# A second queue for the QKV weight loads, a K product tile by tile, ten warm-ups for eighteen, and a new order on every engine

## The chip, the core and the metric

The kernel runs on one core of one Trainium2 chip. The metric is the device time of one execution in microseconds (us). The kernel before was run three times; the number to compare with is the median. One more execution was profiled, and all rows of the profile come from that one.

Five engines work side by side, each through its own queue in order: TensorE (PE, with its weight loads PEld), VectorE (DVE), ScalarE (ACT), GpSimd (POOL) and SyncE (SP), which here only issues DMAs. An instruction that waits holds up everything behind it on its engine.

## The reference

Two rounds of one attention layer and one MLP layer with the same weights in both rounds, on x of 1 x 2048 x 512 (S = 2048 rows, D = 512), all in bf16:

```python
    x = A_x
    x = x + _A_ref(_layernorm(x, axis=-1), A_wqkv, A_wo)
    x = x + _B_ref(_layernorm(x, axis=-1), B_w1, B_b1, B_w2, B_b2)
    x = x + _A_ref(_layernorm(x, axis=-1), A_wqkv, A_wo)
    x = x + _B_ref(_layernorm(x, axis=-1), B_w1, B_b1, B_w2, B_b2)
```

`_A_ref` projects to q, k and v with wqkv (512 x 1536), takes 32 heads of 16, lets each row see itself and the 255 rows before it, takes the softmax, multiplies by v and projects with wo. `_B_ref` is gelu(x w1 + b1) w2 + b2 with 1792 hidden columns.

## The kernel before, in words

The rows are cut into tiles of 128, and the two rounds together give 32 tiles ("tau", 0 to 31), or 16 attention blocks of two tiles ("b", 0 to 15; 0 to 7 is the first round). X stays in SBUF for the whole kernel. All weights are loaded once.

For each block, `lnq` (L672) normalizes its two tiles: statistics on DVE (`bs`, `ba`, L616 and L618), the variance plus eps (`vp`, L622, on POOL or DVE), a power on POOL (`pw`, L628), and the scaling on DVE (`xn`, L638). The normalized tile is transposed into xnTA, for the first four tiles and the last two by PE (`tp`, L650) with a copy out of PSUM on ACT or DVE (`te`, L605 to L607), and otherwise by a DMA transpose on SP (`tx`, L643). Then `proj` (L684) makes Q and K (`q0_0` is block 0, first half of the columns; each such product is four nodes of two matmuls of 256 columns, 128x256), and `kv` (L691) copies K to KT with a mask on DVE (`ke`, L698) and makes V (`v`, four matmuls of 512 columns for a tile). Q and V are copied by DVE or ACT (`qe`, `ve`, L605 to L607). Two DMAs on SP shift V by half a tile (`vs`, L713).

`attention` (L741) works in "visits" of 512 score columns for four row groups: scores on PE (`sc`, L765), two exponentials of 128x1024 on ACT (`ex`, L772), masks on DVE or POOL (`mk`, L793). A block has ten visits (five at the start of a round), 150 in all. Then come the product with V (`pv`, L817), a transpose, a reciprocal and a scaling (`od`, `rc`, `nm`, L826 to L834), another transpose (`ot`, L840) and the output projection (`op`, L861, added to X by `rs`, L866). `mlp` (L870) works in jobs of two or four tiles: W1 products (`m`), a bias on DVE and a gelu on ACT (`gb`, `ga`) or both on ACT (`ge`, L897), the W2 products (`y`) and the sum into X (`ya`, L909). Exponentials and gelus need different tables on ACT; each change of table is a load of 1.28 us.

The code records about 3,080 "nodes" with what each reads and writes (`_Plan.add`, L391). What runs in which order is written out by hand: `_ORDER` (L167) lists all nodes in one order, which gives the order on each engine; `_ALT` (L323) names the nodes that run on their second engine (a copy on ACT instead of DVE, a mask on POOL instead of DVE); `_TURNS` (L342) adds pairs in which one node has to wait for another; `_BANKS` (L362) gives each product its PSUM bank. `_Sched.op` (L62) turns each node into an instruction with semaphore waits. DMAs take turns on eight semaphores (L73 to L79), and a DMA on a semaphore waits until the one before it there has landed.

The loads at the start all stand on SP. In the recorded order they are issued as: X tile 0, X tile 1, X tiles 2 and 3, K weights first half (256 KB), b1, Q weights first half, X tiles 4 to 7 (512 KB), K weights second half, V weights (512 KB), Q weights second half, X tiles 8 to 11, X tiles 12 to 15, b2, Wo. W1 and W2 come later, between other DMAs.

Eighteen warm-up matmuls of 128x512 on a tile of zeros (L555 to L558) keep PE busy: fifteen of them before the first projection product, the other three between the products of blocks 0 and 1.

## Time and profile before

| | us |
|---|---|
| median of three runs | 440.32 |
| lowest and highest of them | 439.97 and 440.69 |
| the profiled execution | 440.62 |
| its span in the profile | 438.9 |
| PE busy, ACT busy, DVE busy, POOL busy in it | 424.2, 385.6, 341.0, 201.1 |

How to read it: times in rows are microseconds from the start of the span, and the means of one instruction are nanoseconds. A row of the timeline has its start, its length, the engine, the line of the kernel, the operation, the tile it writes and those that it reads, the count, and in brackets the idle time of the engine ahead of it with what ended it. A row of a group has its total busy time and the mean of one, then the idle time ahead of the group with what ended most of it. The profile's granted clock (PEclk) is 1.00 in all stretches but the last one of 20 us (0.97). PE's busy time holds the latency of each matmul too, so that a PE busy 100% isn't a PE at its peak.

### The profile page before, as it was taken

What the parts mean: (1) busy time and instruction counts of PE and PEld (TensorE: products, weight loads), DVE (VectorE), ACT (ScalarE), POOL (GpSimd) and SP (SyncE); (2) the same over time, 40 slices, a digit from 0 to 9 for tenths busy, and PEclk for the clock granted to TensorE, in tenths of its full rate; (3) what the DMA queues carried; (4) which work ended last, traced back from release to release, by engine and by line L of the source; (5) the groups of instructions that cost most, each with busy time, mean ns of one, the idle gap of its engine ahead of it and who ended that gap; (6) DMA issues with size and microseconds to landing.
All of it is one profiled execution on the core that took longest, in us unless ns stands there. A gap on an engine that the chain in (4) does not pass through costs nothing.

```text
span 438.9 us, 16940 instructions
## 1 busy us (share of the span) xinstructions
PE 424.2 (97%) x7579; PEld 230.4 (52%) x7579; DVE 341.0 (78%) x647; ACT 385.6 (88%) x457; POOL 201.1 (46%) x224
## 2 busy tenths in 40 slices
PE   8989999999699989999999999999999999999997
PEld 4555756554344554454455555454564554544763
DVE  5999987799686889876899797877877686754852
ACT  3899999999999899999999988899888979899632
POOL 4366136464550275451854437743454515625222
PEclk9999999999999999999999999999999999999999
DMA  7772912002200102311030211201232022101011
GB/s 236 210 203 50 227 39 56 15 21 64 48 1 14 32 16 48 50 33 25 10 74 9 37 29 27 52 1 33 58 45 69 1 33 63 47 0 28 15 48 49
DMA packets 47972, 23.25 MB, mean 53 GB/s; under 512 B 33180, under 2 KB 47900, under 8 KB 47900
## 3 DMA queue, kind: packets, MB, share of 16 engines
q1 hardware_dynamic: 47900, 22.17, 21.8%
q8 instruction: 60, 0.98, 0.9%
q14 instruction: 12, 0.10, 0.1%
HBM read 8.00 MB, written 2.10 MB: 23 GB/s over the span
## 4 chain that ended last, share of the span: by engine, by line
PE 84%; ACT 8%; DVE 4%; DMA 3%; issue 1%; SPq 1%; POOL 0%; DVEq 0%
PE ps L664 65%; PE ps L765 10%; PE ps L817 8%; ACT E L772 7%; DMA W_sb<-in_B_w_dram 1%; DMA xnTB<-xn 1%; DVE stat L616 1%; DVE OD L826 1%; DVE KT L698 1%; DMA X<-in_A_x_dram 0%; PE ps L650 0%; DVE xn L638 0%; DVE X L909 0%; DVE X L866 0%; SPq L643 0%
## 5 line engine op out<-in xcount | busy, mean ns | idle before, releaser
L772 ACT ACTIVATE E<-ps 128x1024 bf16<-128x1024 f32 x300 | 283.2, 1040 | 25.6 <-PE ps L765 24.8
L793 POOL TENSOR_TENSOR E<-E,mask 128x512 bf16<-128x512 bf16 (+2 forms) x114 | 120.3, 1069 | 132.5 <-ACT E L772 52.7
L664 PE MATMUL ps<-W_sb,gT 128*128 128x512 bf16 x448 | 114.8, 380 | 0.1
L664 PE MATMUL ps<-xnTB,W_sb 128*128 128x512 bf16 (+1 forms) x560 | 109.3, 337 | 1.9 <-ACT E L772 1.5
L664 PEld LDWEIGHTS ps<-xnTB,W_sb 128*128 128x128 bf16 x560 | 51.9, 98 | 43.4 <-issue 4.6
L664 PE MATMUL ps<-xnTA,Wqkv_sb 128*128 128x256 bf16 x512 | 71.6, 273 | 1.2 <-ACT E L772 0.9
L765 PE MATMUL ps<-QT,KT 32*128 32x128 bf16 (+3 forms) x1920 | 60.4, 231 | 4.6 <-ACT E L772 2.6
L664 PEld LDWEIGHTS ps<-W_sb,gT 128*128 128x128 bf16 x448 | 39.4, 98 | 42.8 <-issue 4.0
L793 DVE TENSOR_TENSOR E<-E,mask 128x512 bf16<-128x512 bf16 (+2 forms) x122 | 51.0, 445 | 13.8 <-ACT E L772 11.6
L664 PEld LDWEIGHTS ps<-xnTA,Wqkv_sb 128*128 128x128 bf16 x512 | 46.6, 98 | 22.6 <-issue 3.3
L765 PEld LDWEIGHTS ps<-QT,KT 32*128 32x128 bf16 x1920 | 28.4, 92 | 52.6 <-ACT E L772 34.5
L826 DVE STREAM_TRANSPOSE OD<-ps 128x1024 f32<-128x1024 f32 x32 | 40.0, 1249 | 16.5 <-PE ps L817 14.6
L897 ACT ACTIVATE gT<-ps,b1T 128x512 bf16<-128x512 f32 (+1 forms) x80 | 43.0, 606 | 9.1 <-PE ps L664 9.0
L889 DVE TENSOR_SCALAR gT<-ps,b1T 128x512 bf16<-128x512 f32 (+1 forms) x60 | 36.7, 631 | 11.9 <-PE ps L664 11.4
L616 DVE BATCH_NORM_STATS2 stat<-X 128x6 f32<-128x512 bf16 x64 | 43.6, 687 | 3.0 <-DMA X<-in_A_x_dram 2.2
L905 POOL TENSOR_TENSOR Xb<-X,b2all 128x512 f32<-128x512 bf16 x32 | 36.8, 1154 | 13.1 <-DVE X L909 6.4
L817 PE MATMUL ps<-E,Va 64*17 64x256 bf16 (+3 forms) x1920 | 41.0, 230 | 1.8 <-DVE Va L605 0.5
L698 DVE TENSOR_TENSOR KT<-ps,parmask 128x1024 bf16<-128x1024 f32 x32 | 38.7, 1213 | 5.2 <-PE ps L664 5.0
L817 PE MATMUL ps<-E,Vs 64*17 64x192 bf16 (+3 forms) x1920 | 42.2, 230 | 0.0
L628 POOL TENSOR_TENSOR rstd<-rstd,mhalf 128x2 f32<-128x2 f32 (+1 forms) x33 | 24.2, 734 | 27.6 <-DVE rstd L622 23.3
L817 PEld LDWEIGHTS ps<-E,Va 64*17 64x17 bf16 x1920 | 29.2, 84 | 11.9 <-issue 8.3
L664 PE MATMUL ps<-Wo_sb,OT 128*128 128x512 bf16 x128 | 35.3, 380 | 0.1
(51 smaller groups left out, 350.1 us busy)
## 6 DMA issues: line engine op xcount, KB each, us to landing
Vs<-Va SPq DMA_DIRECT2D x64, 68.0 KB, 2.7
W_sb<-in_B_w_dram SPq DMA_DIRECT2D x4, 512.0 KB, 4.6
out_dram<-X SPq DMA_DIRECT2D x16, 128.0 KB, 1.8
X<-in_A_x_dram SPq DMA_DIRECT2D x3, 512.0 KB, 7.9
Wqkv_sb<-in_A_wqkv_dram SPq DMA_DIRECT2D x4, 256.0 KB, 5.5
W_sb<-in_B_w_dram SPq DMA_DIRECT2D x1, 768.0 KB, 5.2
W_sb<-in_B_w_dram SPq DMA_DIRECT2D x2, 384.0 KB, 5.0
Wqkv_sb<-in_A_wqkv_dram SPq DMA_DIRECT2D x1, 512.0 KB, 7.7
```

The source lines that it names most:

```text
L616: add("dve", lambda e, B, t=t, k6=k6: e.bn_stats(stat6[:, k6, :], X[:, t, :]), reads=["X%d" % t], writes=["st%d" % k6], key="bs%d" % (k + j))
L628: add("pool", lambda e, B, j=j, n=n: e.tensor_tensor(out=rstd[:, k + j : k + j + n], in0=rstd[:, k + j : k + j + n], in1=mhalf[:, 0:n], op ...
L664: r = e.matmul(ps[:, B[g][0], cols], lhsT, rhs, start=st, stop=sp)
L698: add("dve", lambda e, B, g=g, i=i: e.tensor_tensor(out=KT[:, kb, 2 * i : 2 * i + 2].rearrange("p c m a q -> p a (c m) q"), in0=ps[:, B[g] ...
L765: x = e.matmul(ps[:, bk[r], o : o + n], KT[rows, kb, c, m].rearrange("p a q -> p (a q)"), QT[rows, c, q : q + n], start=True, stop=True)
L772: add("act", lambda e, B, g_=g_, gi=gi: e.activation(E[:, 2 * gi : 2 * gi + 2, e0 : e0 + 512], ps[:, B[g_][0] : B[g_][0] + 2, :], AF.Exp, ...
L793: fn = lambda e, B: e.tensor_tensor(out=Ew, in0=Ew, in1=Mw, op=ALU.mult)
L817: x = e.matmul(ps[32 * r : 32 * r + VW, B[g][par], c % 2 * 2 * P + lo : c % 2 * 2 * P + hi], V[rows, (2 * b + m // 2) % VR, c * HC + 2 * r ...
L826: add("dve", lambda e, B: e.transpose(OD[:, s].rearrange("p a c q -> p (a c q)"), ps[:, B[g][0] : B[g][0] + 2, :]), reads=["ps:" + g], wri ...
L889: add("dve", lambda e, B, g=g, fc=fc: e.tensor_scalar(out=gT[:, fc, c0 : c0 + M], in0=ps[:, B[g][0], 0:M], scalar1=b1T[:, fc : fc + 1], sc ...
L897: add("act", lambda e, B, g=g, fc=fc: e.activation(gT[:, fc, c0 : c0 + M], ps[:, B[g][0], 0:M], AF.Gelu_apprx_tanh, bias=b1T[:, fc : fc + ...
L905: add("pool", lambda e, B, t=t, xs=xs: e.tensor_tensor(out=Xb[:, xs, :], in0=X[:, t, :], in1=b2all[:], op=ALU.add), reads=["X%d" % t, "b2a ...
```

## The change

Four things are changed together.

First, `load_w` puts the five QKV weight loads on ACT's queue. In the new order they are K first half, Q first half and K second half, all three ahead of ACT's first table load; then Q second half between the copies `te0` and `te1`; then V between `te1` and `te3`. Each has a semaphore of its own (`actdma0` and so on), so that none waits for an earlier one; the K load first waits for the memset of gT. SP now issues X tile 0, tile 1, tiles 2 and 3, tiles 4 to 7, b1, tiles 8 to 11, tiles 12 to 15, b2, Wo.

Second, the first K product (`k0_0`) is cut by tile: four nodes of four matmuls with 128 columns, of which the first two need tile 0 of xnTA alone. `k0_0` now comes ahead of `q0_0`, whose products in before stood in between.

Third, NWARM is 10: eight warm-ups ahead of the first transposes, one after each of the first two tiles' transposes, and none later.

Fourth, `_ORDER`, `_ALT`, `_TURNS` and `_BANKS` are replaced. At the start, DVE now has the statistics of tiles 2 and 3 ahead of `xn1`, and the statistics of tile 4 (`bs4`) ahead of the copy `te2`. By engine: copies of Q on ACT 8 for 11, copies of V on ACT 15 for 14; masks on DVE 127 for 122, on POOL 109 for 114; `nm` on POOL 15 for 13; `vp` on POOL 22 for 16. Both orders have 18 table loads on ACT.

```diff
-    COUNTERS = ("pe", "act", "dve", "pool") + tuple("spdma%d" % i for i in range(8))
+    N_ACT_DMA = 8
+    COUNTERS = ("pe", "act", "dve", "pool") + tuple("spdma%d" % i for i in range(8)) + tuple("actdma%d" % i for i in range(8))
...
         if dma:
-            assert eng == "sp"
-            counter = "spdma%d" % (self.dma_rr % self.N_DMA_SEMS)
-            self.dma_rr += 1
             inc = 16
-            prev = self.cnt_val[counter]
-            if prev > 0:
-                need(counter, prev)
+            if eng == "act":
+                assert self.act_dma < self.N_ACT_DMA
+                counter = "actdma%d" % self.act_dma
+                self.act_dma += 1
+            else:
+                assert eng == "sp"
+                counter = "spdma%d" % (self.dma_rr % self.N_DMA_SEMS)
+                self.dma_rr += 1
+                prev = self.cnt_val[counter]
+                if prev > 0:
+                    need(counter, prev)
...
-    NWARM = 18
+    NWARM = 10
...
-        def dma(fn, writes, reads=(), key=None):
-            return add("sp", fn, reads=reads, writes=writes, dma=True, key=key)
+        def dma(fn, writes, reads=(), key=None, eng="sp"):
+            return add(eng, fn, reads=reads, writes=writes, dma=True, key=key)
...
-                ["Wqkv%d_%d" % (which, i) for i in range(2) if lo <= D // 2 * i < lo + n], key="ldw%d_%d" % (which, lo))
+                ["Wqkv%d_%d" % (which, i) for i in range(2) if lo <= D // 2 * i < lo + n],
+                reads=["g0_0"] if (which, lo) == (1, 0) else (), key="ldw%d_%d" % (which, lo), eng="act")
...
-        def proj(g, which, i, xs, xr, war):
+        def proj(g, which, i, xs, xr, war, first=False):
+            if first:
+                for n in range(4):
+                    j, half = divmod(n, 2)
+                    kc = 2 * i + half
+                    pe_group(g, [(Wqkv_sb[:, dc, which * D + kc * P : which * D + (kc + 1) * P],
+                                  xnTA[:, xs, dc, j * P : (j + 1) * P],
+                                  slice(half * 256 + j * P, half * 256 + (j + 1) * P), dc == 0, dc == DC - 1)
+                                 for dc in range(DC)],
+                             DC, [xr[j], "Wqkv%d_%d" % (which, i)], fresh=(n == 0), war=war, key=g, k0=n)
+                return
...
-                proj(g, 1, i, xs, xr, names)
+                proj(g, 1, i, xs, xr, names, b + i == 0)
```

## The prediction

> **What bounds the kernel now.** I read the page's busy shares first, then its chain of waits, then a table by stretches, then the costliest groups.

> ```profile
> PE 424.2 (97%) x7579; PEld 230.4 (52%) x7579; DVE 341.0 (78%) x647; ACT 385.6 (88%) x457; POOL 201.1 (46%) x224
> PE 84%; ACT 8%; DVE 4%; DMA 3%; issue 1%; SPq 1%; POOL 0%; DVEq 0%
> 0.00:20.00 20.00, 18.19 (x157) 10.04 (x157) 15.55 (x36) 11.58 (x15) 8.16 (x25) 1.00 0.81 237
> 20.00:40.00 20.00, 18.43 (x450) 10.86 (x450) 18.90 (x34) 19.52 (x24) 10.78 (x12) 1.00 0.50 133
> 100.00:120.00 20.00, 15.52 (x424) 8.78 (x427) 16.21 (x29) 19.28 (x23) 9.42 (x12) 1.00 0.27 58
> 380.00:400.00 20.00, 20.00 (x204) 8.70 (x187) 10.17 (x20) 19.30 (x24) 7.94 (x9) 1.00 0.01 2
> L772 ACT ACTIVATE E<-ps 128x1024 bf16<-128x1024 f32 x300 | 283.2, 1040 | 25.6 <-PE ps L765 24.8
> ```

> TensorE is busy 97% of the span and ScalarE 88%. The chain runs through PE for 84% and ACT for 8%. The stretches (columns: length, then busy time of PE, PEld, DVE, ACT, POOL, then granted clock, DMA share and GB/s) say where each rules. From 380 to 400 us PE has no idle time. From 100 to 120 us it lacks 4.48 us while ACT is busy 19.28 of 20. The 300 exponentials make up most of ACT's time. The chain in order of time says the same:

> ```profile
> 106.68 11.92 ACT E L772 x13
> 126.60 11.62 PE ps L664 x57
> 422.33 13.47 PE ps L664 x90
> ```

> Thirteen exponentials stand back to back in 11.92 us, 0.92 us each. So the first layer is led by ACT in places, and the end is bare PE work. Time is won only by starting the exponentials earlier, by taking work off ACT in the early stretches, or by taking work off PE.

> **The change part by part.** The base is the profiled execution: 440.62 us, of which 438.9 is the span. It lies 0.30 us above the median of 440.32, so I subtract from the median at the end.

> *The start.* The rows of before, in order of time:

> ```profile
> 0.79 1.34 SPq L565 DMA_DIRECT2D X<-in_A_x_dram  x3
> 1.24 4.29 PE L557 MATMUL ps<-gT 128*128 128x512 bf16 x10 [1.24 <-DVE gT L555]
> 2.81 0.69 DVE L616 BATCH_NORM_STATS2 stat<-X 128x6 f32<-128x512 bf16 x1 [1.63 <-DMA X<-in_A_x_dram]
> 4.24 2.32 SPq L570 DMA_DIRECT2D Wqkv_sb<-in_A_wqkv_dram  x3
> 6.11 1.08 ACT L607 ACTIVATE xnTA<-ps 128x512 bf16<-128x512 bf16 x2 [4.05 <-PE ps L650]
> 6.35 1.03 PE L557 MATMUL ps<-gT 128*128 128x512 bf16 x4
> 7.25 0.99 PEld L664 LDWEIGHTS ps<-xnTA,Wqkv_sb 128*128 128x128 bf16 x10 [0.37 <-ACT xnTA L607]
> 7.79 0.73 DVE L638 TENSOR_SCALAR xn<-X,statmv,rstd 128x512 bf16<-128x512 bf16 x2 [0.75 <-POOL rstd L628]
> 9.02 2.60 PE L664 MATMUL ps<-xnTA,Wqkv_sb 128*128 128x256 bf16 x22
> 9.22 0.42 DVE L605 COPY xnTA<-ps 128x512 bf16<-128x512 bf16 x1 [0.16 <-PE ps L650]
> 10.17 0.69 DVE L616 BATCH_NORM_STATS2 stat<-X 128x6 f32<-128x512 bf16 x1 [0.53 <-DMA X<-in_A_x_dram]
> 12.04 0.40 PE L765 MATMUL ps<-QT,KT 32*128 32x256 bf16 x8 [0.42 <-DVE KT L698]
> 12.60 0.59 PE L664 MATMUL ps<-Wqkv_sb,xnTA 128*128 128x512 bf16 x2
> ```

> The first projection product waits for ACT's copy of xnTA at 7.25, not for weights. So weights that come sooner free nothing there by themselves. ACT issues five loads: three ahead of its table load, one between the copies te0 and te1, one between te1 and te3. ACT is idle for 4.05 us before 6.11, which hides the first three (2.32 us for three is the longest such group on SP). The other two stand where ACT waits for the next transposes; I take 0 for them, up to 0.8 us if one takes long, as SP's three did.

> The tile-by-tile K product has 16 matmuls of 128 columns and as many weight loads, for 8 of 256. Ten loads took 0.99 us, 0.10 each, so eight more cost up to 0.8 us; half of them run while PE waits for tile 1 anyway, and the rest stands where the next wait is DVE's. I take 0.

> What decides is the new order on DVE. In before, tile 2's copy te2 (9.22) stands ahead of the statistics that wait for the load of tiles 4 to 7 (10.17). In after, such a statistic, bs4, stands ahead of te2, and PE's q1_0 and k1_0 (sixteen of the 22 matmuls of the 9.02 row, 16/22 x 2.6 = 1.9 us less the overlap of their ends, 1.75) wait for te2. The first scores come behind them. If that load is early, bs4 starts when xn2 and xn3 end, near 8.9 (xn1 now follows two statistics, so the row of 7.79 moves 0.4 back): scores at 8.9 + 0.69 + 0.42 + 1.75 = 11.76, or 0.3 us before the 12.04 of before. If the load lands at L, they come at L + 0.69 + 0.42 + 1.75.

> ```profile
> 0.00:9.00 9.00, 7.61 (x42) 3.74 (x43) 5.28 (x18) 2.59 (x4) 5.37 (x19) 1.00 0.72 212
> 4.70:6.50 1.80, 1.65 (x13) 0.78 (x12) 1.80 (x6) 0.39 (x1) 0.97 (x4) 1.00 0.66 160
> 9.00:11.60 2.60, 2.60 (x26) 1.99 (x23) 1.92 (x4) 1.57 (x3) 0.00 (x0) 1.00 1.12 342
> Wqkv_sb<-in_A_wqkv_dram SPq DMA_DIRECT2D x1, 512.0 KB, 7.7
> ```

> When it is saturated, the DMA moves 342 GB/s, 0.34 MB per us; from 4.70 to 6.50 only 160, as SP hadn't issued enough. In before, the load landed at 10.17 with 1.54 MB issued up to and with it. In after, 1.02 MB of SP's own stand there, and the 0.77 MB of ACT's first three loads share the engines: 1.79 MB, 0.25 MB or 0.75 us more; filling the gap of 4.70 to 6.50 gives back 1.8 x 0.18 / 0.34 = 0.95. So L = 10.0 and the scores start at 12.85: **0.8 us late**. Bounds: 0.3 early (load in time), 3.5 late (rival 1).

> [...]

> *Warm-ups.* Eight fewer. Five of them stood at the start, where PE waits. Three stood between the products of the first layer:

> ```profile
> 19.81 0.38 PE L557 MATMUL ps<-gT 128*128 128x512 bf16 x1
> 21.34 0.38 PE L557 MATMUL ps<-gT 128*128 128x512 bf16 x1
> 31.08 0.39 PE L557 MATMUL ps<-gT 128*128 128x512 bf16 x1
> ```

> Four in a row take 1.03 us with the last one's tail (row of 6.35), 0.22 each without it; three are 0.65. PE has 1.57 us of idle time from 20 to 40, which hides some of it: I take **-0.4** (bounds -0.65 and 0).

> *Searched order.* The recorded orders differ everywhere, yet engine by engine little is moved: 18 table loads in both, and nearly the same PE work ahead of each exponential. Copies move from ACT to DVE:

> ```profile
> L607 ACT ACTIVATE Va<-ps 128x512 bf16<-128x512 f32 x14 | 8.7, 623 | 0.3 <-PE ps L664 0.2
> L607 ACT ACTIVATE QT<-ps 128x512 bf16<-128x512 f32 x11 | 6.8, 619 | 0.8 <-PE ps L664 0.8
> L605 DVE CAST QT<-ps 128x512 bf16<-128x512 f32 x21 | 14.3, 682 | 5.2 <-PE ps L664 5.1
> L793 DVE TENSOR_TENSOR E<-E,mask 128x512 bf16<-128x512 bf16 (+2 forms) x122 | 51.0, 445 | 13.8 <-ACT E L772 11.6
> ```

> Ahead of the 50th exponential, ACT has 12 copies for 15, three by 0.62, 1.86 us less, all in the stretch where it is busy 19.5 of 20 or close to that. DVE takes them for 3 x 0.68 = 2.0 us; it was busy 18.90 of 20 from 20 to 40 us, so this is not free. I take **-1.4** (bounds -1.86 and 0), near the full sum, as ACT's share there is the higher one. Over the whole run ACT has two copies fewer; DVE gets five masks more, 5 x 0.445 = 2.2 us by the last row above, and gives six small variance steps to POOL. I cost these at 0, as DVE has 22% idle time over the span; if they all fell where it is busy 18.90 of 20, they would cost up to 2.2.

> What else the new order does to stalls can't be worked out from the trace. Its bounds are the 4.48 us of PE idle from 100 to 120 us, all closed or once more opened; I take 0.

> Sum: +0.8 - 0.4 - 1.4 = -1.0, that is 439.6 on the profiled execution, and from the median 440.32 - 1.0 = **439.3**. The bare PE work of the end (13.47 us) has the same matmuls in both.

> **The rivals.**

> 1. *V's weights come last (slower).* In after the V load (512 KB) is ACT's fifth, issued only behind te1, beside SP's 2.69 MB of X, b2 and Wo. PE meets its first V product right after the first scores (12.60 in before), and the second scores stand behind it. In before it landed 7.7 us after an issue near 4.75, at 12.45: just in time. If SP's loads are all served first, 3.97 MB stand up to it for 2.30 in before: 1.67 / 0.34 = 4.9 us more, less 0.95, so 4.0 later, 16.4. It costs nothing up to 13.4 (0.8 late like the scores), and from 15.3 on, 2.7 late, it outweighs the 1.8 us won and the bound of 0.9. At 16.2 the second scores are 3.6 late: 440.32 + 3.6 - 1.8 = 442.1. For it: two rings, and a load that is issued late. Against it: equal shares put it near 13.1. Chance 0.20.

> 2. *The new order closes holes.* If 60% of the 4.48 us goes, -2.7: 439.3 - 2.7 = 436.6. For it: PE idle there waits for ACT, which has less work. Against it: ACT is busy 19.28 of 20 in that very stretch. Chance 0.18.

> 3. *The clock.* The ten first warm-ups took 0.43 us each, the four from 6.35 0.22 each, though the granted clock in the rows is 1.00 throughout: PE doubles its pace after some 4.3 to 5 us of work. Eight warm-ups end at 1.24 + 8 x 0.43 = 4.7, and PE then idles until the first transposes. If the pace stays at half until the scores, 24 matmuls of 256 columns cost 0.11 us more each: 2.6 us, 439.3 + 2.6 = 441.9, slower too. [...] Chance 0.10.

> 4. *It does not do what it says.* The loads free nothing (row of 7.25), and DVE gives back what ACT saves, as the chain is PE's: +0.8 - 0.4 = 440.7. Chance 0.12.

> **How the numbers follow.** Forecast 439.3, chance 0.40, its own range 438.2 to 440.7 by the bounds of the copies and the start. Faster by over 0.2% means below 439.44, slower above 441.2; 0.2% is about what a measurement of this kernel can tell from no change. Faster: 0.24 of the forecast and rival 2's 0.18 = 0.42. Same: 0.16 of the forecast, 0.01 of rival 1, 0.06 of rival 4 = 0.23. Slower: 0.19 + 0.10 + 0.06 = 0.35. The range 436.4 to 442.6 leaves out the lower part of rival 2 (0.07) and the upper parts of rivals 1 and 3 (0.11).

> **What would show it.** Start: the first scores at 12.85, with te2 behind a statistic that waits for X; at 11.7 the load came early. Rival 1: the first V product waits for Wqkv_sb beyond 13.4. Rival 3: projection products of 128x256 spaced by 0.21 us instead of 0.11. Copies: the 50th exponential earlier by 0.8 us or more against the first. Rival 2: PE busy above 18 of 20 in every stretch from 80 to 180. I am wrong where stalls of several us stand in stretches that this text doesn't name.

## The result, and the profile after

The changed kernel takes **445.96 us** (median of six runs, 444.37 to 448.7), beside 440.5 for the kernel before on the same chip (439.65 to 442.5). The ratio is 1.0123 [1.0083, 1.0163]: 5.5 us slower, and outside the range of 436.4 to 442.6. The profiled execution took 444.37 us with a span of 442.5.

The page of the changed kernel: busy time, and the costliest group.

```profile
PE 423.7 (96%) x7579; PEld 230.7 (52%) x7579; DVE 341.3 (77%) x646; ACT 384.6 (87%) x455; POOL 199.1 (45%) x227
L790 ACT ACTIVATE E<-ps 128x1024 bf16<-128x1024 f32 x300 | 283.6, 1038 | 26.8 <-PE ps L783 26.0
```

The work is the same: as many matmuls as before, the same time in them, the same exponentials. So the 3.6 us that the span is longer by (442.5 for 438.9) are waits, or matmuls spaced further apart. The table by stretches of the changed kernel says where (length, busy PE, PEld, DVE, ACT, POOL, granted clock, DMA share, GB/s):

```profile
0.00:20.00 20.00, 14.65 (x106) 8.77 (x107) 12.89 (x31) 8.15 (x11) 8.19 (x23) 0.91 0.75 220
100.00:120.00 20.00, 16.52 (x487) 9.60 (x470) 17.54 (x33) 19.36 (x23) 9.90 (x12) 1.00 0.36 55
380.00:400.00 20.00, 20.00 (x254) 9.02 (x250) 13.18 (x24) 17.69 (x22) 5.78 (x6) 1.00 0.07 19
```

From 0 to 20 us PE is busy 14.65 us for 18.19, ACT 8.15 for 11.58, and the granted clock is 0.91 for 1.00. In the other two PE is as busy as before or busier, at a clock of 1.00. ACT's table loads are good milestones, since both kernels have 18 of them at the same places of the work. The second and the last, in before and then in the changed kernel:

```profile
46.22 1.28 ACT L897 ACT_TABLE_LOAD   x1
408.07 1.28 ACT L897 ACT_TABLE_LOAD   x1
49.52 1.28 ACT L915 ACT_TABLE_LOAD   x1
412.81 1.28 ACT L910 ACT_TABLE_LOAD   x1
```

That is 3.3 us late at 46 us and 4.7 at 408, and the span ends 3.6 late: nearly everything is lost before 46 us. The timeline of that start (start, length, engine, line, operation, tiles, count, and in brackets the idle time ahead with its releaser):

```profile
6.10 1.29 DVE L624 BATCH_NORM_STATS2 stat<-X 128x6 f32<-128x512 bf16 x2 [0.75 <-DMA X<-in_A_x_dram]
9.08 0.19 PE L597 MATMUL ps<-ident,b1raw 14*128 14x14 bf16 x1 [0.71 <-DMA b1raw<-in_B_b_dram]
9.20 1.89 PE L672 MATMUL ps<-xnTA,Wqkv_sb 128*128 128x128 bf16 x14
11.98 0.42 DVE L613 COPY xnTA<-ps 128x512 bf16<-128x512 bf16 x1 [1.25 <-PE ps L658]
14.33 0.40 PE L783 MATMUL ps<-QT,KT 32*128 32x256 bf16 x8
16.21 0.82 PE L672 MATMUL ps<-Wqkv_sb,xnTA 128*128 128x512 bf16 x3 [1.48 <-DMA Wqkv_sb<-in_A_wqkv_dram]
17.61 0.40 PE L783 MATMUL ps<-QT,KT 32*128 32x256 bf16 x8
```

Read it from the top. DVE waits until 6.10 for X tiles 2 and 3. Then PE, with the rest of the K product queued behind it, waits until 9.08 for b1, 3.5 KB. The next 14 matmuls (the last twelve of the K product, of 128 columns, and two of the Q product) take 1.89 us; in the run below with the loads back on SP the same 14 take 1.27. So te2 waits for PE's transposes, and not for a statistic. The first scores come at 14.33 for 12.04. Then V's weights land, at 16.2, and the second scores come at 17.61, where they stood at 13.78 before: 3.8 us late.

Two rows of a shorter table of the changed kernel, and landings in the DMA view (KB each, median us from issue to landing), V and X tiles 2 and 3 in the changed kernel, then X tiles 2 and 3 in before:

```profile
4.70:6.50 1.80, 0.75 (x7) 0.29 (x6) 1.01 (x4) 0.60 (x1) 0.88 (x2) 1.00 1.11 344
9.00:11.60 2.60, 2.52 (x22) 2.37 (x23) 1.42 (x4) 0.05 (x1) 0.26 (x1) 0.50 1.11 337
```

```profile
Wqkv_sb<-in_A_wqkv_dram ACTq DMA_DIRECT2D x1, 512.0 KB, 8.0
X<-in_A_x_dram SPq DMA_DIRECT2D x1, 256.0 KB, 4.4
X<-in_A_x_dram SPq DMA_DIRECT2D x1, 256.0 KB, 2.8
```

The gap that the prediction wanted filled is filled: 344 GB/s from 4.70 to 6.50 for 160. But X tiles 2 and 3, which took 2.8 us to land before, now take 4.4. And from 9.00 to 11.60 the granted clock is 0.50. In before the rows show 1.00 even over the slow first warm-ups (0.43 us each, for 0.22 from 6.35 on), and I had not counted on seeing a slow clock in them; here the row shows it.

### The profile page after: what moved, and what is told of

It reads as the page before. It is cut to its first block, busy times and chain, and to the rows that moved or that the text cites. A ratio compares the mean times of both kernels' runs of the same rounds, so it can differ in the third digit from the quotient of the medians.

```text
span 442.5 us, 16952 instructions
## 1 busy us (share of the span) xinstructions
PE 423.7 (96%) x7579; PEld 230.7 (52%) x7579; DVE 341.3 (77%) x646; ACT 384.6 (87%) x455; POOL 199.1 (45%) x227
## 3 DMA queue, kind: packets, MB, share of 16 engines
q10 hardware_dynamic: 2640, 1.57, 1.2%
## 4 chain that ended last, share of the span: by engine, by line
PE 58%; DMA 1%; ACT 1%; DVE 1%; issue 0%; SPq 0%
PE ps L672 46%; PE ps L783 6%; PE ps L835 5%; DMA xnTB<-xn 1%; ACT E L790 1%; DVE E L811 0%; DVE xn L646 0%; DVE X L927 0%; DVE Va L613 0%; DVE QT L613 0%; PE ps L658 0%; SPq L134 0%
## 5 line engine op out<-in xcount | busy, mean ns | idle before, releaser
L811 POOL TENSOR_TENSOR E<-E,mask 128x512 bf16<-128x512 bf16 (+2 forms) x109 | 115.8, 1074 | 130.1 <-ACT E L790 55.2
L672 PE MATMUL ps<-W_sb,gT 128*128 128x512 bf16 x448 | 113.5, 380 | 0.1
L672 PE MATMUL ps<-xnTA,Wqkv_sb 128*128 128x256 bf16 (+1 forms) x520 | 71.3, 274 | 1.7 <-ACT E L790 0.6
L811 DVE TENSOR_TENSOR E<-E,mask 128x768 bf16<-128x768 bf16 (+2 forms) x127 | 53.0, 442 | 12.7 <-ACT E L790 5.0
L672 PEld LDWEIGHTS ps<-xnTA,Wqkv_sb 128*128 128x128 bf16 x520 | 47.9, 99 | 20.6 <-issue 3.5
L907 DVE TENSOR_SCALAR gT<-ps,b1T 128x512 bf16<-128x512 f32 (+1 forms) x60 | 37.7, 634 | 12.9 <-PE ps L672 12.0
L672 PE MATMUL ps<-Wqkv_sb,xnTA 128*128 128x512 bf16 x128 | 34.7, 381 | 1.7 <-DMA Wqkv_sb<-in_A_wqkv_dram 1.5
## 6 DMA issues: line engine op xcount, KB each, us to landing
W_sb<-in_B_w_dram SPq DMA_DIRECT2D x4, 512.0 KB, 4.7
X<-in_A_x_dram SPq DMA_DIRECT2D x3, 512.0 KB, 7.6
Wo_sb<-in_A_wo_dram SPq DMA_DIRECT2D x1, 512.0 KB, 11.4
```

Source lines behind the costliest of these rows:

```text
L672: r = e.matmul(ps[:, B[g][0], cols], lhsT, rhs, start=st, stop=sp)
L811: fn = lambda e, B: e.tensor_tensor(out=Ew, in0=Ew, in1=Mw, op=ALU.mult)
L907: add("dve", lambda e, B, g=g, fc=fc: e.tensor_scalar(out=gT[:, fc, c0 : c0 + M], in0=ps[:, B[g][0], 0:M], scalar1=b1T[:, fc : fc + 1], sc ...
```

## The experiments

Theory T1: with two queues, loads that aren't needed yet (X 8 to 15, b2 and Wo on SP) share the DMA engines with the urgent ones, so that X 2 and 3, b1 and V's weights all land late. T2: PE falls to half its pace at the start, as it has too few warm-ups. T3: the searched order costs elsewhere. A fourth, T4, came up in the second group. Ratios are against the kernel before on the same chip, whose medians were 440.56 to 441.16.

### First group: the loads, the clock, the order

**All loads back on SP** (a1_sp_loads):

```diff
-                reads=["g0_0"] if (which, lo) == (1, 0) else (), key="ldw%d_%d" % (which, lo), eng="act")
+                key="ldw%d_%d" % (which, lo))
```

> The changed kernel with the five weight loads back on SP in the order of before; everything else as changed. Theory 1 (two queues share the DMA engines, so X tiles 2 and 3, b1 and V's weights land late): X tiles 2 and 3 land before 5 us, V's weights near 12.5, the first scores start near 13.0 (14.33 in the changed kernel), the second near 14.4 (17.61), and about 3 of the 3.7 us come back: ratio to before 1.000 to 1.004. Theory 2 (PE's clock falls to half in the idle start, for lack of warm-ups): the clock row still shows about 0.5 from 9 to 11.6, and at most 1 us comes back. Theory 3 (the searched order costs elsewhere): nothing comes back, ratio near 1.010.

Measured: 441.48 us, ratio 1.0005 [0.9989, 1.0021]. First and second scores in its timeline, and its 9 to 11.6 us:

```profile
12.33 0.40 PE L793 MATMUL ps<-QT,KT 32*128 32x256 bf16 x8
14.06 0.40 PE L793 MATMUL ps<-QT,KT 32*128 32x256 bf16 x8
```

```profile
9.00:11.60 2.60, 1.87 (x19) 1.43 (x17) 2.20 (x5) 1.14 (x3) 0.82 (x4) 1.00 1.12 347
```

Order, K product by tile and ten warm-ups together cost nothing, and the clock stays at 1.00. The loads make the loss. T3 falls, and so does T2 as a cause of its own: the same ten warm-ups do no harm here.

**The loads on ACT alone** (b1_act_loads): the kernel before, with the five loads on ACT at the changed kernel's places and SP's loads in the order of before, so b1 ahead of X 4 to 7.

```diff
-                ["Wqkv%d_%d" % (which, i) for i in range(2) if lo <= D // 2 * i < lo + n], key="ldw%d_%d" % (which, lo))
+                ["Wqkv%d_%d" % (which, i) for i in range(2) if lo <= D // 2 * i < lo + n],
+                reads=["g0_0"] if (which, lo) == (1, 0) else (), key="ldw%d_%d" % (which, lo), eng="act")
```

> The kernel before with only the five weight loads moved to ACT's queue, in the changed kernel's places, and SP's loads in its own order without them. Theory 1: V's weights land near 16 and the second scores start near 17.3 (13.78 in before): 3 us slower, ratio 1.006 to 1.009. Theory 2: all eighteen warm-ups are there, so at most 0.5 us slower. Theory 3: no difference.

Measured: 447.22 us, ratio 1.0148 [1.0124, 1.0171], the whole loss and more. Its timeline, and a row of its table:

```profile
6.21 0.69 DVE L630 BATCH_NORM_STATS2 stat<-X 128x6 f32<-128x512 bf16 x1 [1.06 <-DMA X<-in_A_x_dram]
17.69 1.49 PE L678 MATMUL ps<-Wqkv_sb,xnTA 128*128 128x512 bf16 x3 [3.83 <-DMA Wqkv_sb<-in_A_wqkv_dram]
```

```profile
16.00:19.00 3.00, 1.31 (x4) 0.61 (x6) 0.00 (x0) 0.00 (x0) 0.00 (x0) 0.50 0.06 19
```

X 2 and 3 are late again, and PE waits 3.83 us for V's weights. This kernel has eighteen warm-ups, and yet its clock is 0.50 from 16.00 to 19.00, behind that wait: here the slow clock stands behind an idle PE, and eighteen warm-ups haven't kept it away. PE doesn't wait for b1 in this kernel.

**X 8 to 15 held back** (a2_x_last): the changed kernel, whose SP waits for V's weights before X 8 to 11 and all behind it.

```diff
-                ["X%d" % t for t in range(t0, t0 + n)], key="ldx%d" % t0)
+                ["X%d" % t for t in range(t0, t0 + n)], reads=["Wqkv2_0"] if t0 == 8 else (), key="ldx%d" % t0)
```

> The changed kernel with X tiles 8 to 15, b2 and Wo issued only once V's weights have landed. Theory 1: V's weights no longer share with them and land near 11.5 (16.2 in the changed kernel), so the second scores start near 15.3 instead of 17.61; X tiles 2 and 3 still share with K's and Q's weights and land near 6.1, so the first scores stay near 13.8 to 14.3. About 2.3 us come back: ratio 1.004 to 1.007. Theory 2: first scores at 14.3 and clock 0.5 as before, gain under 0.5 us. Theory 3: none.

Measured: 443.51 us, ratio 1.0061 [1.003, 1.0092], half of the loss back. In its timeline the first scores are the row at 12.78 and the second the one at 14.51; the last row is V's landing:

```profile
5.67 1.29 DVE L634 BATCH_NORM_STATS2 stat<-X 128x6 f32<-128x512 bf16 x2 [0.42 <-DMA X<-in_A_x_dram]
8.77 0.18 PE L607 MATMUL ps<-ident,b1raw 14*128 14x14 bf16 x1 [0.82 <-DMA b1raw<-in_B_b_dram]
12.78 0.40 PE L793 MATMUL ps<-QT,KT 32*128 32x256 bf16 x8
14.51 0.40 PE L793 MATMUL ps<-QT,KT 32*128 32x256 bf16 x8
```

```profile
Wqkv_sb<-in_A_wqkv_dram ACTq DMA_DIRECT2D x1, 512.0 KB, 3.8
```

V lands in 3.8 us for 8.0, and PE doesn't wait for it. b1 is still late. The weights on the second queue aren't the whole reason: in the changed order b1 also stands behind X 4 to 7 (512 KB) on SP itself. By the packets in the traces its transfer ends at 8.30 in the changed kernel, at 6.30 in b1_act_loads, where it stands ahead of X 4 to 7, and at 5.11 in before. The clock of this execution is 1.00 at the start, and its first scores are only 0.7 us late.

**More warm-ups** (a3_fill): six more in PE's idle time between 5 and 9 us of the changed kernel.

```diff
-    NWARM = 10
+    NWARM = 16
```

> The changed kernel with six more warm-ups in PE's three idle times between 5 and 9 us. Theory 2: the clock row stays near 1.0 from 6.5 to 11.6, the first scores start 0.8 to 1.5 us earlier and the whole gains 1 to 1.5 us. Theory 1: the clock may stay up and the first scores come 0.5 to 1 us earlier, but V's weights still land at 16.2 and hold the second scores at 17.6: the whole gains less than 0.3 us, and the spread from run to run may shrink. Theory 3: no gain.

Measured: 448.96 us, ratio 1.0187 [1.0162, 1.0211]. In its timeline:

```profile
12.88 0.40 PE L793 MATMUL ps<-QT,KT 32*128 32x256 bf16 x8
17.03 0.59 PE L682 MATMUL ps<-Wqkv_sb,xnTA 128*128 128x512 bf16 x2 [3.76 <-DMA Wqkv_sb<-in_A_wqkv_dram]
```

The first scores come 1.45 us sooner than in the changed kernel, as T2 says, and then PE stands until V's weights have landed. So the half pace at the start was hidden behind V. That this kernel came out slower still, by 3 us, no theory said. Held against the changed kernel, its table loads are 0.6 us later at 50.08, 1.1 at 79.70, 2.1 at 134.76 and 3.4 at 398.89. Between the second and the third its clock is 0.58 and 0.56 (124 to 128 us), where the changed kernel's is 1.00. Ahead of the fourth its weight loads wait 1.23 us, at 388.88, where the changed kernel has no such wait: six warm-ups are twelve instructions more, and the third group below shows what that can do.

### Second group: the parts one by one

**V alone back on SP** (c1_v_on_sp):

```diff
-                key="ldw%d_%d" % (which, lo), eng="act")
+                key="ldw%d_%d" % (which, lo), eng="sp" if which == 2 else "act")
```

> The changed kernel with only V's weight load moved back to SP's queue, directly behind b1; the other four loads stay on ScalarE's queue. It splits the loss of the changed kernel (5 us against before) into V's late landing and the rest. If X tiles 2 and 3 and b1 landing late make the loss (first scores 2.3 us later than before), the first scores stay near 14.3, the second scores stand 1.7 behind them at 16.0 instead of 17.6, and the time is 2 us under the changed kernel at most: 443.5 to 444.5. If V's place as fifth load on ScalarE makes nearly all of it, the time comes to 440.5 to 441.5. If two queues as such cost (searched order, clock), it stays at 445 to 446.

Measured: 444.34 us, ratio 1.0099 [1.0067, 1.013]. In its timeline:

```profile
14.25 0.40 PE L793 MATMUL ps<-QT,KT 32*128 32x256 bf16 x8
15.99 0.40 PE L793 MATMUL ps<-QT,KT 32*128 32x256 bf16 x8
```

First scores as late as in the changed kernel, second scores 1.6 us sooner: 1.6 us are V's, and the other 2.2 come from X 2 and 3, b1 and the slow clock (0.50 from 9.00 to 11.60 here too).

**te2 first** (c2_te2_first): a1 with te2 ahead of the statistics of tile 4.

```diff
 _ORDER, nodes on DVE
-    bs4, te2
+    te2, bs4
```

> The changed kernel with all five loads back on SP in the order of before, and the copy te2 ahead of the statistics of tile 4 on DVE, which waited 0.83 us for X with te2 behind it. If the start leads, the second half of the first products and the first scores come 0.8 us earlier, at 11.5 for 12.33, and the time falls by 0.5 to 0.9 us below the version with the statistics first (441.48), to 440.6 to 441.0, which is the time of before or 0.4 under it. If what is gained is lost again where the exponentials wait for other things, it stays at 441.5.

Measured: 441.45 us, ratio 1.0013 [0.9996, 1.003]. Its first exponential starts 0.86 us sooner than in a1, and the end isn't measurably better than before.

**Ten warm-ups alone** (b2_ten_warm), in the kernel before:

```diff
-    NWARM = 18
+    NWARM = 10
```

> The kernel before with ten warm-up matmuls for eighteen and nothing else (eight ahead of the first transposes, one behind each of the first two). If the clock theory holds for this part, PE falls to half its pace in the idle stretches up to 12 us, the granted clock of 9 to 11.6 us shows 0.5 and the time rises by 1 to 2.6 us, to 442 to 443.5. If the loads alone make the loss, it is within 0.5 us of before (440.5 to 441.5); the prediction's term, three late warm-ups for 0.4 us, would put it at 440.6 where before is at 441.0.

Measured: 442.18 us, ratio 1.0038 [1.0023, 1.0052]. Its table:

```profile
6.50:9.00 2.50, 2.15 (x11) 1.29 (x10) 1.38 (x8) 0.77 (x2) 0.92 (x2) 0.67 1.05 330
9.00:11.60 2.60, 2.60 (x21) 2.08 (x20) 1.01 (x3) 0.91 (x2) 0.00 (x0) 0.66 1.12 342
```

The clock dips to 0.67, and the first scores come 1.1 us late. This kernel also has sixteen instructions fewer on PE; how much of its 1.6 us that makes isn't separated here. In the changed kernel with the loads in time (a1), the same ten warm-ups leave the clock at 1.00 from 9.00 to 11.60.

**The K product by tile alone** (b3_k_tiles), in the kernel before:

```diff
-                proj(g, 1, i, xs, xr, names)
+                proj(g, 1, i, xs, xr, names, b + i == 0)
```

> The kernel before with the first K product cut by tile and set ahead of the Q product, and nothing else. The prediction put it at 0; the eight more matmuls and weight loads of 128 columns cost at most 0.8 us. If it frees PE early, the first scores come up to 0.4 us earlier (11.6 to 12.04); otherwise they stand where they stood. 440.6 to 441.4 by all theories, as the first scores wait for te2 and K's copy. A time over 442 would say that this part has a share in the loss.

Measured: 445.52 us, ratio 1.0112 [1.0084, 1.014]. All theories said 441. Its start is that of before (first scores at 12.07). The loss comes later, at waits of PE's weight loads, two of which end with nothing in particular ("issue"):

```profile
12.07 0.40 PE L784 MATMUL ps<-QT,KT 32*128 32x256 bf16 x8
53.23 0.99 PEld L673 LDWEIGHTS ps<-W_sb,gT 128*128 128x128 bf16 x6 [1.58 <-ACT gT L916]
107.04 0.64 PEld L673 LDWEIGHTS ps<-Wqkv_sb,xnTA 128*128 128x128 bf16 x4 [1.39 <-issue]
385.48 5.29 PEld L673 LDWEIGHTS ps<-xnTB,W_sb 128*128 128x128 bf16 x26 [1.70 <-issue]
```

```profile
q8 instruction: 60, 0.98, 0.9%
```

Sixty packets with 0.98 MB are 16 KB each; if all are PE's, that is, by my estimate from these two counts, a block of about 250 instructions for some 15,200 matmuls and weight loads. T4 supposes: where a block is used up by short matmuls before the next has landed, PE stands. Sixteen instructions more (eight matmuls and their weight loads) would then move the ends of all later blocks.

### Third group: blocks of PE's program

**Sixteen more instructions that do nothing** (d1_pad16), in the kernel before:

```diff
-    NWARM = 18
+    NWARM = 26
...
-            add("pe", lambda e, B, bk=h % 8: e.matmul(ps[:, bk, :], gT[:, 0, 0:P], gT[:, 0, :], start=True, stop=True),
+            add("pe", lambda e, B, bk=h % 8, w=16 if 10 <= h < 18 else 512: e.matmul(ps[:, bk, :w], gT[:, 0, 0:P], gT[:, 0, :w], start=True, stop=True),
```

> The kernel before with eight more warm-up matmuls of only 16 columns behind its first ten, where TensorE waits for the first normalized tile anyway: 16 more instructions on TensorE ahead of everything else, and no other change. [...] Cutting the K product by tile adds 16 instructions too and cost 5 us with an unchanged start; so this kernel should show the same stalls, 1.4 us near 105 and 1.7 us near 383, each with nothing that it waits for, and take 442.5 to 445.5. If the K product by tile costs by its own matmuls or by its place, this kernel takes 440.4 to 441.0, as before does.

Measured: 447.17 us, ratio 1.0129 [1.0106, 1.0153]. Eight matmuls of 16 columns, where PE waits anyway, cost 6 us. In its timeline the start is unchanged and the two stalls stand where b3 has them; its table shows the clock behind the first:

```profile
11.99 0.40 PE L774 MATMUL ps<-QT,KT 32*128 32x256 bf16 x8
107.83 0.32 PEld L673 LDWEIGHTS ps<-Wqkv_sb,xnTA 128*128 128x128 bf16 x2 [2.06 <-issue]
388.96 0.98 PEld L673 LDWEIGHTS ps<-xnTB,W_sb 128*128 128x128 bf16 x6 [1.97 <-issue]
```

```profile
107.00:109.00 2.00, 1.17 (x4) 0.54 (x4) 1.51 (x3) 0.64 (x1) 1.02 (x1) 0.72 0.00 0
109.00:111.00 2.00, 2.00 (x18) 0.72 (x17) 0.00 (x0) 0.67 (x2) 0.13 (x1) 0.50 0.00 0
```

Behind this stall of 2.06 us the clock is 0.50 from 109.00 to 111.00, and it costs more than its length: the table loads on both sides of it are 1.6 us late at 82.42 (80.83 in before) and 4.5 at 132.99 (128.52), 2.9 us more. The slow clock isn't there behind every stall: behind the one of 1.97 us at 388.96 in the same execution the clock stays at 1.00, and so it does behind the longest of e4 below (2.64 us, row of 109 to 111). As in b3, a third wait stands at 53 us. The DMA view of 386 to 387.8 us holds one packet, of the instruction queue, at 5.2% of 16 engines' 1.8 us, or 1.5 us:

```profile
q8 instruction: 1, 0.02, 5.2%
```

No other DMA runs there, and PE goes on at 388.96, some 1.4 us behind the end of that packet.

The other traces bear this out. Behind the first 15 us, and apart from a place at 117 to 127 us, the twenty profiles of this document hold fourteen waits of the weight loads of 1 us or more that end on "issue" and with no DMA landing just ahead. Each ends 1.2 to 1.5 us behind the end of a 16 KB instruction packet, while such packets come some 7 us apart on average. All fourteen stand in the six kernels that add instructions to PE (a3, b3, d1 and, below, e2, e4 and f1), and none in the others, which have as many as before or fewer. At 117 to 127 us all twenty, before included, have one wait of 1.4 to 2.3 us. It ends 1.1 to 1.6 us behind such a packet too, but in sixteen profiles also 0.06 us behind the landing of a DMA transpose (xnTB) that the product reads, so what it waits for isn't settled.

**K by tile and ten warm-ups** (d2_k_ten): b2's and b3's edits in one kernel, 16 instructions more and 16 fewer.

```diff
-    NWARM = 18
+    NWARM = 10
...
-                proj(g, 1, i, xs, xr, names)
+                proj(g, 1, i, xs, xr, names, b + i == 0)
```

> The kernel before with the K product by tile and ten warm-ups for eighteen: 16 instructions more and 16 fewer, so that TensorE's later program stands where it stood in before. The block theory: the stalls near 105 and 383 us are gone, and what is left is the slower start of the ten warm-ups alone (442.2): 441.5 to 442.7, at least 3 us below the K product by tile alone (445.5). If each part has a cost of its own, they add: 445.5 + 1.6 = 447.

Measured: 441.8 us, ratio 1.001 [0.9993, 1.0027]. Parts that cost 1.0112 and 1.0038 alone cost nothing measurable together: the stalls at 53, 107 and 385 us are gone, and the mean clock of the profiled execution is 1.00, where b2's is 0.66 from 9.00 to 11.60.

**K whole, loads on SP** (d3_whole_k): c2 without its K product by tile.

```diff
-                proj(g, 1, i, xs, xr, names, b + i == 0)
+                proj(g, 1, i, xs, xr, names)
```

> The changed order with all loads on SP, the copy te2 ahead of the statistics of tile 4, ten warm-ups, and the first K product whole: 16 instructions fewer than the same version with the K product by tile (441.45). Block theory: its stalls with nothing to wait for (0.53 us near 44 and 0.76 near 383) move or go, and the time changes by up to 1.5 us without a change of the start; where they go, 440.0 to 440.8. If the K product by tile helps the start, the first scores come 0.3 us later than 11.5 and the time is 441.7.

Measured: 443.36 us, ratio 1.0043 [1.0025, 1.0061]. Its first scores come at 12.02, about 0.55 us behind those of c2, and the rest of the 1.9 us isn't explained. T4 had no way to tell the sign.

**The gate, with b1 late** (d4_gate_b1, then e1_gate_b1_later): a2 with te2 first, and the transpose of b1 behind k1_0, then behind v0.

```diff
 _ORDER, nodes on PE
-    tp1, b1t, k0_0.1, ..., k1_0.3, sc0_0
+    tp1, k0_0.1, ..., k1_0.3, b1t, sc0_0
```

> The changed kernel with two queues kept, X tiles 8 to 15, b2 and Wo held on SP until V's weights have landed (443.51 so far), the transpose of b1 moved behind the last K product of block 0, and te2 ahead of the statistics of tile 4. If the wait for b1 (0.82 us on TensorE) and the statistics are what is left at the start, the first scores come at 11.5 to 12.0 for 12.78 and the time falls by 0.8 to 1.2 us, to 442.3 to 442.7. If what is left stands later (the loads of X 8 to 15 and W1, now 5 us later, or blocks of TensorE's program), it stays at 443 to 443.6.

Measured: 445.21 us, ratio 1.0095 [1.0072, 1.0118]. The first scores came at 12.26, but the first V product waited 1.59 us for the PSUM bank of b1, which my edit had made them share. Mended in e1, where b1t stands behind v0 with another bank:

> The version with the gate on X tiles 8 to 15 (two queues, te2 ahead of the statistics of tile 4), with the transpose of b1 behind the first V products and in a PSUM bank that is free for long: in the version before this one the first V product waited 1.59 us for the bank of b1. If that wait alone made it slow, the second scores come 1.6 us earlier, at 14.0 for 15.65, and the time falls from 445.2 to 442.5 to 443.7, so that two queues with the gate are still 1 to 2 us behind one queue. If the gate's late X tiles cost by themselves, it stays over 444.

Measured: 443.67 us, ratio 1.0055 [1.0035, 1.0075], like a2. The wait is gone, yet its first scores came only at 13.63, as the clock of this execution was low:

```profile
9.00:11.60 2.60, 2.60 (x22) 2.25 (x20) 1.01 (x4) 0.60 (x1) 0.30 (x2) 0.52 0.75 204
```

Two queues with a gate are still 0.5% behind one queue. Why the rest stays isn't settled. In a2 a part of it stands at 45.79, where the weight loads wait 1.54 us: the DMA transpose of xnTB that they read landed only at 45.73, 4.4 us after its issue, for 3.2 in a1.

### Fourth group: T4 tried harder

**Thirty-two at the start** (e4_pad32): as d1 with sixteen matmuls of 16 columns.

> The kernel before with sixteen more matmuls of 16 columns at the start (32 instructions on TensorE) where eight cost 6 us. If each such matmul costs by itself, it takes twice as much: 452 to 454. Block theory: the ends of all blocks move by 32 instructions instead of 16, so the stalls change in size and place but don't double: 441 to 448, with the first scores where they were (12.0) and the loss, if any, only behind stalls of TensorE that wait for nothing shown.

Measured: 454.71 us, ratio 1.0311 [1.0284, 1.0337]: more than twice d1's loss, which is what I had put down for a cost of each matmul, and outside what I gave T4. Only the trace told them apart. Its first scores come at 12.27 for 12.04, so the sixteen matmuls cost little where they stand, and the timeline has these stalls among others:

```profile
54.56 0.77 PEld L674 LDWEIGHTS ps<-xnTB,W_sb 128*128 128x128 bf16 x8 [2.25 <-issue]
110.02 0.11 PEld L775 LDWEIGHTS ps<-QT,KT 32*128 32x128 bf16 x6 [2.64 <-issue]
306.42 0.99 PEld L674 LDWEIGHTS ps<-xnTA,Wqkv_sb 128*128 128x128 bf16 x10 [1.54 <-issue]
394.05 0.09 PEld L827 LDWEIGHTS ps<-E,Vs 64*17 64x17 bf16 x3 [2.32 <-issue]
```

Its table loads fall back where the stalls are: 3.6 us late against before at 56.14 and still 3.6 at 78.51, 7.9 at 136.44, 11.4 at 392.55 and 13.8 at 404.60.

**The same at 197 us** (e2_pad_late): the small matmuls inside the Q product of block 9. They stand in both halves, sixteen in all and not eight, and the second eight overwrite 16 columns of that product.

```diff
-                def fn(e, B, part=part):
+                def fn(e, B, part=part, pad=8 if (g, i) == ("q9_0", 0) else 0):
+                    for _ in range(pad):
+                        e.matmul(ps[:, B[g][0], 0:16], part[0][0], part[0][1][:, 0:16], start=True, stop=True)
```

> The kernel before with eight more matmuls of 16 columns (16 instructions on TensorE), this time inside the first Q product of block 9, between 180 and 200 us; their results are overwritten by the product itself. Block theory: up to there nothing changes (no stall near 105, where the same 16 instructions at the start made one of 2.06 us), and behind it the stall near 383 comes (1.97 us with the 16 at the start, some 2.0 us of delay): 442.6 to 443.6. If the eight matmuls cost by themselves wherever they stand (6 us at the start), it takes 445 to 447; if only the start matters, 441.2.

Measured: 447.17 us, ratio 1.0147 [1.0115, 1.0179]. As it has thirty-two instructions, it is to be held against e4: the stalls behind 197 us are e4's, and those at 55 and 110 are missing.

```profile
298.12 0.99 PEld L675 LDWEIGHTS ps<-xnTA,Wqkv_sb 128*128 128x128 bf16 x10 [1.54 <-issue]
385.92 0.09 PEld L828 LDWEIGHTS ps<-E,Vs 64*17 64x17 bf16 x3 [2.48 <-issue]
```

**The clean form** (f1_pad_late8): eight, in the first half only (`(g, i, k0) == ("q9_0", 0, 0)`).

> The kernel before with eight more matmuls of 16 columns inside the first half of the first Q product of block 9, near 197 us, overwritten by that product itself (the version before this one had them in both halves, sixteen in all, and the second eight overwrote 16 columns of the first half's result). Block theory: nothing changes up to 197 us; behind it TensorE's blocks lie as with eight at the start, so that the stall near 383 us (1.97 us there) comes and the others (297, 420) don't: 442.6 to 443.6. A cost of 0.75 us for each such matmul would give 446.6 to 447.2.

Measured: 443.09 us, ratio 1.0045 [1.003, 1.006], 2.4 us over before (440.72), inside what T4 said and 3.5 us under the least that a cost per matmul would give. The one new stall over 1 us is the one expected:

```profile
382.34 5.29 PEld L675 LDWEIGHTS ps<-xnTB,W_sb 128*128 128x128 bf16 x26 [1.22 <-issue]
```

The profiled execution is the fastest of the ten (441.51 us), and its table loads are 0.8 us late behind that stall, so the rest of the 2.4 us isn't seen in it. What costs, then, is not the matmul itself; the cost fits T4, by which it is the place where a block ends. That the stalls wait for the block is inferred from the packets ahead of their ends; no run changed the loading itself. In before, at most one packet of the sixty is followed by such a wait of 1 us, the one of 1.64 us that ends at 118.66; e4 has five besides that one, the longest of 2.64 us.

**K whole in the changed kernel** (e3_after_whole_k), the diff of d3 on the changed kernel:

> The changed kernel with the first K product whole, as in before; loads, order and ten warm-ups stay changed. It undoes one part. If the loads on two queues make the loss, the first scores stay later than 13.5, V's weights land near 16, and the time stays between 445 and 448 (16 instructions fewer may move it by 1 to 2 us either way). If the K product by tile has a share of its own in the loss, it falls under 444.

Measured: 446.35 us, ratio 1.0135 [1.0107, 1.0164], as slow as the changed kernel. Its first scores come at 15.54, 1.2 us behind those of the changed kernel, and its second at 17.61 like them, as both wait for V.

**No late warm-ups** (f2_no_late): the kernel before with `NWARM = 15`, the three at 19.8, 21.3 and 31.1 us left out.

> The kernel before without its three late warm-ups (19.8, 21.3 and 31.1 us), the fifteen at the start kept: 6 instructions fewer on TensorE. The prediction's term gives 0.4 us (0 to 0.65) less: 440.2 to 440.6 where before is at 440.6 to 441.2. If TensorE's waits there hide them, no change. Block theory: 6 instructions move the ends of blocks by a third of what cost 6 us in the other direction, so that a change of up to 2 us either way that starts behind 40 us would speak for it.

Measured: 440.8 us, ratio 0.9996 [0.9983, 1.0009]. Its second table load comes at 46.27 for 46.22.

## Why the prediction was wrong, point by point

- **The start, +0.8: the step that failed.** The first scores came 2.3 us late and the second 3.8, where 0.8 was forecast. I worked out one landing with equal shares by bytes issued, X 4 to 7 at 10.0. It landed at 8.8 (issued at 2.18, 6.6 us by the DMA view), and the statistic behind it started at 10.04 only because DVE came to it then, so that this figure looks right by luck. X 2 and 3 and b1 were left where they had been, and V was made a rival. All three stood beside more bytes in flight, b1 behind 512 KB more of its own queue as well, and each is waited for ahead of the first or second scores. Some 1.5 us of the 2.3 are the slow clock behind those waits: a2 and a3, whose clock is 1.00 up to 11.60, have the first scores at 12.78 and 12.88. The 0.7 or 0.8 that is left equals the forecast, but through other loads, which is luck too. The step "weights that come sooner free nothing there by themselves" was right; that sooner weights make X later was missing.
- **Rival 1 (V last)** had the mechanism and the size: V at 16.2 for a worst case of 16.4, second scores 3.8 late for 3.6. The closeness is partly luck, as its sum left out Q's second half: 4.22 MB stand up to V and not 3.97, which by the same working gives 17.1. I gave it 0.20, since equal shares put V at 13.1; they didn't hold for a load issued at 8.20, behind all the others. Its time of 442.1 was too low, because 1.8 us of gains were set against it that didn't come; without them it is 443.9, still 2.1 short.
- **Warm-ups, -0.4:** not seen. f2's ratio of 0.9996 has an interval that still holds -0.4 us (0.9991), but its second table load, behind all three, comes no sooner. PE's waits there may have hidden them.
- **Copies, -1.4:** not seen. In a1, whose first exponential starts 0.28 us later than in before, the table load of 46.22 comes at 46.03: 0.5 us are won by then. The next one but one, 74.94 in before, comes at 74.89, and the whole run is even (1.0005). The sign that I had named, the 50th exponential 0.8 us earlier against the first, isn't there: 61.08 us behind it for 61.41 in before.
- **K by tile, 0:** right in this kernel (e3), by luck: what it wins at the first scores there is lost in the wait for V. Alone it costs 5 us (b3), as T4 has it through sixteen instructions, and eight warm-ups fewer give them back (d2). I had counted the durations of instructions and not their number.
- **Searched order, 0 within 4.48:** right as far as a1 can tell, which holds it together with the K product and the warm-ups.
- **Rival 3 (clock):** the slow clock was there, with 0.50 from 9.00 to 11.60, but as a result of PE's waits for late loads: with the loads on SP, ten warm-ups leave it at 1.00 (a1). Ten warm-ups alone, with the loads in time, cost 1.6 us (b2).

Between a1 (441.48, all loads on SP) and the changed kernel (445.96) lie 4.5 us in the medians, but only 2.4 in the two profiled executions. The changed kernel's six runs lie between 444.37 and 448.7, with a mean granted clock of 0.995 or 0.996 in the four up to 446.11 and of 0.992 in the two above. So I take a part of the rest for the clock; no run tests this. No version beat the kernel before.

## What to carry to other kernels

The second DMA queue added no bandwidth where the engines were already full (342 GB/s from 9.00 to 11.60 in before, 337 after); it let loads that can wait share them with loads that can't: V took 8.0 us to land beside X 8 to 15, and 3.8 with them held back (a2). So list every load that is waited for early, the smallest too, and work out each one's landing. This program has a second timeline, its instruction packets, sixty of 16 KB: when an edit adds or removes a few matmuls, look for new waits on "issue" far behind the edit, and try the edit with the number of instructions made up, before you believe its time. Parts that are neutral together can cost alone: 1.1% and 0.4% here.

## What the runs showed of the hardware that was not expected

- Eight matmuls of 16 columns at the start cost 6 us of 441 (d1), sixteen 14 (e4), with first scores within 0.25 us of those of before.
- Fourteen waits of PE's weight loads on "issue", of 1.0 to 2.64 us, end 1.2 to 1.5 us behind the end of a 16 KB instruction packet; all stand in the six kernels that add instructions to PE.
- Behind a PE stall of 2.06 us the granted clock was 0.50 from 109 to 111 us (d1), and behind one of 3.83 us 0.50 from 16 to 19 (b1_act_loads); behind stalls of 1.97 (d1) and 2.64 us (e4) it stayed at 1.00.
- A load of 3.5 KB (b1), issued by SP at 2.69, landed near 9.1 us (its last packet ends at 8.30, PE's wait for it at 9.08), behind 1 MB of X on its own queue and beside the weights on the other.
